# One PSUM tile per head pair for the first quad's transposes, a later first v load, and a last store from ScalarE's queue

## The chip, the cores and the metric

The kernel runs on one core of one Trainium2 chip. The metric is the device time of one execution in microseconds (us): three runs of the kernel before gave 442.17, 441.16 and 441.16, median 441.16. The profile is of one further execution, which took 439.23 us.

## The reference

Attention with a threshold, then a feed-forward layer that takes the largest of three products. Shapes: q, k, v are 8 batches x 8 heads x 576 rows x 64; the layer is 512 to 768 to 512.

```python
scores = scale * np.matmul(q, k.transpose(0, 1, 3, 2))
thresh = np.max(scores, axis=-1, keepdims=True) - tau
scores = np.where(scores >= thresh, scores, -1000000000.0)
attn = np.exp(scores - np.max(scores, axis=-1, keepdims=True))
attn = attn / (np.sum(attn, axis=-1, keepdims=True) + 1e-09)
x = np.matmul(attn, v)            # heads side by side: 4608 x 512
h = np.maximum(np.maximum(x @ w1, x @ w2), x @ w3)
out = h @ w_out
```

## The kernel before

The heads are taken four at a time, a *quad*: two quads per batch, 16 in all. A quad's q and k are loaded with 64 partitions for each of two heads (`load`, line 187); the four heads are a grid of `i` (upper or lower 64 partitions of the loaded tile) and `r` (first or second block of columns). For each quad TensorE transposes q and k (`transposed`, line 256; 64 x 64 pieces, five per `i` for `r` = 0, four for `r` = 1) into a PSUM tile `tp`; ScalarE copies q out with the scale into `qt`, VectorE copies k out into `kt`, and GpSimd makes `qs`, a copy of `qt` with upper and lower 64 partitions exchanged (`swapped`, line 242).

The work on scores goes by *chunks* of 128 query rows (nine per quad, `idx` 0 to 8) and by `r`. For one chunk and `r`: `scores` (line 287) makes 128 x 576 scores by matmuls on the upper and lower 64 rows of the array, `maximum` ("m", line 319, VectorE) finds the row's largest value, `exponents` ("e", line 331, ScalarE) makes the shifted values, and the numerators come from ScalarE ("n") or VectorE ("k") (line 339). A table `MASKED` says which chunks go the VectorE way; there "m" writes a copy `z` to SBUF, else "e" reads the scores in PSUM itself. Chunks 0 to 3 need only `i` = 0 of the transposed tiles, chunks 5 to 8 only `i` = 1 (chunk 4 both); chunks 0, 1, 5 and 6 read `qs` in its partitions 64 to 127 (the swap with x = 1), the others in partitions 0 to 63 (x = 0). The result is divided by the row sum (GpSimd), transposed by DMA (`ptq`), multiplied by v ("O"), and goes into the feed-forward layer ("F", "B") and out.

All PSUM is four tiles, s0 to s3, of two banks each (`bank`, line 183). Whatever is put into one of them has to wait until all readers of what was there before are done.

The order is written out by hand. Every engine's instructions are chained in program order (`_Ordered`, line 83), so an instruction that waits holds all behind it on its engine. `beginning()` (line 720) writes out the first quad; then the string `ORDER` (line 41) is followed letter by letter through `issue` (line 641): S0 to S3 is one chunk's `scores` in that tile, T a transpose of a later quad, "m", "e", "n", "k" as above, "a" and "c" the copies of a later quad's q and k out of PSUM, "q" its swaps, "l" one load, "g" and "z" load and cast of weights, "y" a cast of v, "o" a store. The first chunks are c0, c1 (both with `i` = 0; `r` = 0 of both comes before `r` = 1 of both), then c2 (`idx` 5).

In `beginning()` as it stands: 10 transposes of q for `r` = 0 into s0, 10 of k into s1, each tile holding both `i`, with the two `i` alternating. ScalarE copies q, VectorE k, one `i` at a time; three filling transposes keep TensorE busy (`FILL`); then the scores of c0 go to s0; then k and q of `r` = 1 into s2 and s3, all four of their copies by ScalarE; then the scores of c1 to s1. ORDER goes on with S2 and S3.

The first quad's loads are all issued first: on SyncE's queue q in three parts, then v (two of 256 KB, two of 32 KB); on ScalarE's queue k in three parts. The second quad's loads come with the letters "l" on SyncE's queue, behind v. At the end, the last "ninth" piece of the output (line 533) is copied out by VectorE and stored in two halves by SyncE; the store before it goes by ScalarE's queue (line 527).

Of the kernel before, what the change touches and what calls it, by code (L numbers as in the profile page):

```python
# [32 lines left out]
FILL = 3  # L33
# [8 lines left out]
lS2mS3mlemleS1neT0S2lmeamkmgllS1ekqlgT3T0qnalllncT0emS3cmlqqS2zenyyymS0ttzS1tS2eS3nemmnS0emlS2eememtekmS1eS3  # L42
kmgnltemS0S2eS1nklnmlktmS3gnS2eemS1RkmeT0metlmS2eleS3S1nkmmT3eazyS2emlD0ecmtbD3S1O0tkekmnbO2NRwS3wS1D0ennmqm
tebeS2D3bkS0T1ztmeaqkqO3nqtmneynO2NkwS1wS3nmS0F2S1mT3mgeBRmceD0klS3khebezS2tgF0S1mneBmlkmteD2vbF3S2T0kmBeS1n
aengvmezqS0F3mS2BS0mehrT1tS2neO3mecnnO1pgNttmF2qpkF0wwtrrkBT3zgyF1epaBnvvS3BlzhrS2mlF0RemkS1lnBlS2D3pvqD0pel
mrmppbklO3blO0teNqwpS1zweS2mS3npS0mmmrnF1BevS3T1emckS2emteS0npreptlnpT1S3kpmneptgarS2nmmeeS0pteS1mF3S0rekBmm
pnlpthlelS2kT3trktpS1epqpcmrF0nT3mtnpqpaBeS3S2evS0mF1yS3mnetmeegrBpF2mvT0crBeS1F3knpnhympzlgnenS0mlBqpeS1vmS
2O0O3erprmkNF1ekS2xwS3mmrnF0nqBpBepzplttvreS2ttpS3lptF1mmhnS0mBepzpeF3netrvnS2pmBS1pS0vnmtF2mS3S0rekepnepS1m
emreptBltkuS3upmmS0rF1lltpS2lnneekmmT3rBS0aS2kkueuepO3O1qlpqpmrpmekNeS0wmpxS2mF3F1rknBepeT0hplBcF2T3tnvT0Bta
S1ncF3qS0vBnmF2qyS1BemhrrkemF3S0nBvpF2pmepnpS1vBrmS0yeS3hemS2S1yylmlpF3plmmtleF0BlBkeetevrnF2T1T3vltoaBhT0tp  # L50
S1rapnknqS2F0cmmeS3BeF2pqS1mrBvpF0emS3ntppleBvrF2topytnS1kmmBS3hnS0O1vmlepnO2NeqmrkreeT3qS0xtptwcnnF2S1mmkF3
BlpveprBeS0lmS1ppF2hnmeS3rmpyBS1pnS0plvF3ntlT2mmeBaS1olevF2F3kmeueS2enrkrT0qT1tpBmakcepS1muS2urS0mopT3F1ntyp
pcS3leqkrenS2pppmmrneBS3memlupS0mS2uetetO1O3mnekrknpNwxS2S0S1pmpF3BemnF0mlqetS2kqreBtltpheF3knS1mBvprmF0vppe
S2nrBS3epnS1mrmmF2phS0BF1mveeF3kBS2epvenrBlnhnltS0mS1elolpmtltS3F0F2etypmmBkevyBpeT1rT3vF0ancS1BF2otnhmrS3BF
0kmtlplevrT1pppqpBtnltS2aS1oeT3rvmcS0nneS2meS3mqO1mmO0pppqeNeqkkreF2xwS3BS0pmpnhS1metnemF3F2lBkrlS1vBF0mrpve
npF3eBBhnkpvF2S1T0F3aurkBS0mltleS3rvS1mppmmlpqS2F0S1mtolnS2pqpteeemBrkneepS3ultuS1pmrmS2F0peepS3ymmkkntemeoB
nttS1rS2uuO3kppemmrkeO0leNS1xloT2T0npawS3mF1T0rclBcS2enmF0hprqqpmkeF1tpenBS3tttpntvmBoF2eS0vBmrS3S1yppmhS0mF
2eF3BBemepeF1nkT0vkrBF2vanhS0kBnF3F1mrBvBvppqS2petnS0prlpqrolmlmhnepS3F1mtltolBevleS2S0tmnnetF3pS1BmF0rmlepy
S2evBS3hmF1enT0pkBmcrppnvS2S3O0O1rmnNenpmeS3kxerwF2T1aT0mnBT3cvaF1S0ppBheqqprkplmS2eF3S1BmkvnF2eF0mkuqppBenl
S3S0vtrmtS1lmpprmpptF2S3lT0BtmttelteeocS3kekT1ruumS0aS2nmF1mkqrpS0enpeS3BermmkS2euS3pmuenS0qpO1mpyO2qmerekNp  # L60
xT0newS3cS2mleF1mF0BottpllykpBlhrtkF3pevF1BnnS2nvrmBS0mS3lhF2mpS1lotemyepeBpF0S3lvBnenF2tnS1BrkhmvpmtlypS3F0
F2eermkBBS1eF3vnnT0BrvpprrampypttltthS2S0mmS3emF1T0eS2T3cBpqS0mqS2nevemmyaeS3pmkeO1llktO0NpqpekeF2nxnlT3BF0c
rS3BwlvppmtrS1mnotoF2hS0enBmrpF1vrpqpF3lekBeBpnhF2S0vmT1tlpBS3lS0avmpF1tF2mBrnelekS3evutppmrS0qppS2nS1nmF3mr
mS2peekenpS0BemmeS1rkS2emuS0tlT1ueT3mcknrannpepF2S1mS3qppBmtotlmlttkrrpeueS1qqmS3lO0ueemoeO1opptpkklNwS2lS3x
F0mS1BnemehF2kT3mrcnpBS1F0rvS3BltlpnmF2nepmeveS1pkmBS0httnF3eF2mBrBekF1nS0vrBprvpypppS3nmhemeS2S1F3pF0mmBeBr
T2eS1kvnapS3vF2nS0mnBrmmreS3F1pheS2meeBqpnS0mvmeypS2tpS3etlO1qO0mNpmT3neytF2xtlkkrtnweS0ppT1cramBF3S1Bnehvpp
meS2rF0qqmT3BF1ncveT3ktnBF0vS2mrnarBhppS1lF3T0qppeBmcS1S2ovmF0mneT3naepBvS1S3enF0mkmrkqpqueenF2nS0tmS1T3cpqB
eupurrS3mmottoS0pS1mttneelotpmS2O3mkkO1rNwrpeexpneF0nkpS1S3S2mBemS1euuppmF2erkS3tltlBptmrF0S1lhtpmeyppBeS2mv
O1O3NenmxpS0S2kF1mxemrS3kBF2enF0vBermF1tBhpyppyektBvS2pmF3F0vBkS2BF1nmehS3vrBmtpO0eotpnevO2NkF1S3krmnrpxpxBh
F0S2eBF1mS3F2BnvpmBrS0vS3S1ehemmF2kppmnF0rBvkBF3F1BF2ehBtkvevoF3pptkttO0O1NuprBwS3xS1vmmpeS0ekF2S3pmF1oeBmrB  # L70
okettF0peuokoruoF3uhF2pkkF0hvvruF3pF2F0hppF1pvvF3F2vvF0F1F3hvtovhtF2F0F1F3htvF2voF0O1uvO3NvF2xwF0hF3F1vF0vhF
3F1F0hvF3vvF1F0F3vF1hF0hovF3vF1F0vhF3vvF1vBuuF0BuouoF3uooo
# [31 lines left out]
def kernel(  # L104
# [82 lines left out]
    def load(g, first=False):  # L187
# [276 lines left out]
    def ffn(b, part):  # L464
# [68 lines left out]
        def ninth():  # L533
# [10 lines left out]
            def done():  # L544
# [47 lines left out]
    warm = bank("warm", 3)  # L592
# [41 lines left out]
    line["D"] = [(g, r, part) for part in range(2) for g in range(2) for r in range(2)]  # L634
# [85 lines left out]
    def beginning():  # L720
# [38 lines left out]
        for r in range(2):  # L759
            for x in (1, 0):  # L760
                swap(r, 1, x)
# [45 lines left out]
```

## Time and profile before

| | us |
|---|---|
| median of three runs | 441.16 |
| the profiled execution | 439.23 |
| its span | 437.1 |
| TensorE matmuls busy | 420.2 |
| VectorE busy | 398.9 |
| ScalarE busy | 386.1 |
| GpSimd busy | 289.8 |
| first transpose of q | 4.41 |
| first scores | 6.19 |

Times in the profile are counted from the start of the span; the execution has 2.1 us more around it. PE is TensorE's matmuls, PEld its weight loads, DVE VectorE, ACT ScalarE, POOL GpSimd, SP SyncE; a q behind the name is the engine's own instruction queue, which issues DMAs. In a timeline row the first number is the start, the second the length, then engine, operation, output and inputs, and xN the number of instructions that were merged into the row; a bracket gives the idle time before it and what ended it. Nearly every row has line 92, which is the helper that records instructions, so rows are told apart by their tiles.

### The profile page before, as it was taken

What the parts mean: (1) busy time and instruction counts of PE and PEld (TensorE: products, weight loads), DVE (VectorE), ACT (ScalarE), POOL (GpSimd) and SP (SyncE); (2) the same over time, 40 slices, a digit from 0 to 9 for tenths busy, and PEclk for the clock granted to TensorE, in tenths of its full rate; (3) what the DMA queues carried; (4) which work ended last, traced back from release to release, by engine and by line L of the source; (5) the groups of instructions that cost most, each with busy time, mean ns of one, the idle gap of its engine ahead of it and who ended that gap; (6) DMA issues with size and microseconds to landing.
All of it is one profiled execution on the core that took longest, in us unless ns stands there. A gap on an engine that the chain in (4) does not pass through costs nothing.

```text
span 437.1 us, 14271 instructions
## 1 busy us (share of the span) xinstructions
PE 420.2 (96%) x5313; PEld 305.8 (70%) x5313; DVE 398.9 (91%) x1109; ACT 386.1 (88%) x780; POOL 289.8 (66%) x370
## 2 busy tenths in 40 slices
PE   7769998899999999999999999999999999999995
PEld 5535776567787767767787767777677776777862
DVE  3999999999999999999999999999999999999641
ACT  5999989999999999999999999989999999875422
POOL 3614487898879697577668779768769677554500
PEclk9999999999999999999999999999999999999999
DMA  8999999999999999999999969999999977574602
GB/s 256 306 237 219 294 225 209 237 241 205 184 237 212 229 222 207 201 231 221 196 199 206 213 146 253 175 192 218 237 195 183 222 143 145 120 161 125 177 14 109
DMA packets 212773, 87.45 MB, mean 200 GB/s; under 512 B 185824, under 2 KB 199648, under 8 KB 212704
## 3 DMA queue, kind: packets, MB, share of 16 engines
q1 hardware_dynamic: 212000, 85.69, 94.7%
q8 instruction: 42, 0.69, 0.7%
q10 hardware_dynamic: 704, 0.85, 0.6%
q14 instruction: 27, 0.22, 0.2%
HBM read 34.60 MB, written 9.44 MB: 101 GB/s over the span
## 4 chain that ended last, share of the span: by engine, by line
PE 84%; ACT 6%; DVE 5%; issue 2%; DMA 2%; ACTq 0%; DVEq 0%
PE ph L92 32%; PE sc L92 28%; PE po L92 11%; PE o L92 8%; ACT z L92 4%; PE tp L92 4%; DVE z L92 2%; DVE unused L92 1%; ACT P L92 1%; DMA km<-in_k_dram 1%; DMA qm<-in_q_dram 1%; DVE P L92 1%; ACT qt L92 1%; PE d L92 0%; DVE kt L92 0%
## 5 line engine op out<-in xcount | busy, mean ns | idle before, releaser
L92 POOL TENSOR_SCALAR P<-z,rs 128x576 bf16<-128x576 f32 x252 | 207.5, 837 | 77.7 <-DVE rs L92 34.6
L92 PE MATMUL sc<-kt,qt 64*128 64x256 f32 (+2 forms) x640 | 179.5, 422 | 4.2 <-DVE z L92 2.0
L92 PE MATMUL sc<-kt,qs 64*128 64x320 f32 (+2 forms) x640 | 177.4, 411 | 3.0 <-ACT z L92 1.3
L92 PE MATMUL ph<-xt,w 64*128 64x288 bf16 (+4 forms) x2160 | 171.9, 283 | 0.2
L92 PEld LDWEIGHTS <-w 64*128 64x128 bf16 (+1 forms) x2160 | 124.2, 94 | 34.9 <-issue 7.2
L92 DVE TENSOR_SCALAR_CACHE_REDUCE unused<-sc 128x576 bf16<-128x576 f32 x168 | 123.9, 750 | 4.2 <-PE sc L92 3.1
L92 ACT ACTIVATE z<-sc,nm 128x576 f32<-128x576 f32 x168 | 121.7, 743 | 3.9 <-DVE unused L92 1.5
L92 PEld LDWEIGHTS sc<-kt,qs 64*128 64x128 f32 (+1 forms) x640 | 90.6, 175 | 19.9 <-ACT z L92 7.1
L92 PEld LDWEIGHTS sc<-kt,qt 64*128 64x128 f32 (+1 forms) x640 | 90.3, 175 | 18.5 <-ACT z L92 5.7
L92 ACT ACTIVATE z<-z 128x576 f32<-128x576 f32 x148 | 100.4, 682 | 0.3
L92 ACT ACTIVATE z<-z,nm 128x576 f32<-128x576 f32 x120 | 91.3, 774 | 4.7 <-DVE z L92 4.4
L92 DVE TENSOR_SCALAR_CACHE_REDUCE z<-sc 128x576 f32<-128x576 f32 x120 | 89.3, 752 | 5.1 <-PE sc L92 3.7
L92 DVE SCALAR_TENSOR_TENSOR z<-z 128x576 f32<-128x576 f32 x104 | 81.0, 789 | 0.1
L92 POOL COPY qs<-qt 64x640 f32<-64x640 f32 (+3 forms) x68 | 48.0, 706 | 25.8 <-ACT qt L92 22.5
L92 PE MATMUL po<-wo,hT 64*128 64x512 bf16 (+1 forms) x480 | 53.6, 357 | 0.1
L92 ACT ACTIVATE hm<-ph 128x576 bf16<-128x576 f32 (+4 forms) x54 | 32.1, 595 | 20.0 <-PE ph L92 19.6
L92 DVE TENSOR_TENSOR hm<-ph,hm 128x576 bf16<-128x576 f32 (+4 forms) x54 | 36.9, 684 | 7.9 <-PE ph L92 7.9
L92 PEld LDWEIGHTS <-hT 64*128 64x128 bf16 (+1 forms) x480 | 26.5, 97 | 19.7 <-issue 3.4
L92 DVE TENSOR_TENSOR hT<-ph,hm 128x576 bf16<-128x576 f32 (+4 forms) x54 | 37.1, 687 | 2.3 <-PE ph L92 0.4
L92 PE MATMUL o<-ptq,vb 128*64 128x64 bf16 (+2 forms) x576 | 35.8, 275 | 0.0
L92 PEld LDWEIGHTS <-vb 128*64 128x64 bf16 x576 | 22.5, 111 | 14.9 <-issue 5.8
L92 ACT ACTIVATION_READ_ACCUMULATOR z<-z 128x1 f32 x148 | 29.5, 199 | 0.0
(40 smaller groups left out, 298.4 us busy)
## 6 DMA issues: line engine op xcount, KB each, us to landing
vm<-in_v_dram SPq DMA_DIRECT2D x32, 256.0 KB, 5.1
out_dram<-ob SPq DMA_DIRECT2D x31, 256.0 KB, 3.1
qm<-in_q_dram SPq DMA_DIRECT2D x15, 512.0 KB, 4.8
km<-in_k_dram SPq DMA_DIRECT2D x15, 512.0 KB, 5.5
stage<-in_moe_w_dram SPq DMA_DIRECT2D x9, 512.0 KB, 5.3
ptq<-P SPq DMA_TRANSPOSE x144, 4.3
stage<-in_moe_w_out_dram SPq DMA_DIRECT2D x3, 512.0 KB, 5.3
qm<-in_q_dram SPq DMA_DIRECT2D x16, 64.0 KB, 3.4
```

Of the source, the lines that this page charges most:

```text
L92: ins = fn(*a, **kw)
```

## The change

1. `beginning()` fills a PSUM tile of its own for each of q and k and each `i` for `r` = 0: q and k of `i` = 0 into s2 and s3, q and k of `i` = 1 into s0 and s1; five transposes each, one `i` after the other. Then the scores of c0 and c1 follow one another (s2 and s3), and the first "m" is issued. Then q of `r` = 1 goes into s1 and k of `r` = 1 into s0, again `i` = 0 before `i` = 1. Their copies alternate with "e" of c0 and "m" of c1. All k copies are VectorE's now; before, ScalarE made the two of `r` = 1. The four x = 1 swaps come before the four x = 0 swaps.
2. `ORDER` has the same letters, without the "m", "m", "e" that `beginning()` now issues, and with the tiles renamed throughout (0 with 2, 1 with 3). So its first score, c0 with `r` = 1, goes to s0, the next, c1 with `r` = 1, to s1.
3. The three filling transposes and `FILL` are gone; the warming transposes use s1 instead of s3.
4. The third part of the first q goes by ScalarE's queue, that of k by SyncE's. The first v (four DMAs) is issued behind the second quad's q and k.
5. Of the last two half stores one goes by ScalarE's queue.

```diff
-        for n, src, e in srcs:
+        for n, src, e in (srcs if not first else (("q", q, q2), ("k", k, sync))):
             if first:
                 e.dma_start(out=L[n][:, 10:18], in_=rows_of(src)[:, 1, 0:8])
...
                     for x in range(2):
-                        sync.dma_start(out=rows_out[:, 8, 256 * x:256 * x + 256], in_=ob[64 * x:64 * x + 64])
+                        e = scalar if x == 0 and b == B - 1 else sync
+                        e.dma_start(out=rows_out[:, 8, 256 * x:256 * x + 256], in_=ob[64 * x:64 * x + 64])
...
-    warm = bank("warm", 3)
+    warm = bank("warm", 1)
...
+    first_loads = load(0, first=True)
+
+    def later_loads():
+        for g in range(1, NQ):
+            for n, _ in enumerate(load(g)):
+                if g == 1 and n == 3:
+                    for _ in first_loads:
+                        pass
+                yield
...
-                 l=(None for g in range(1, NQ) for _ in load(g)))
+                 l=later_loads())
...
-        def turn(n, r, where):
-            p = transposed(L, n, r)
-            p.first(where)
-            ps[n, r] = p
+        def turn(n, r, i, to):
+            rows = slice(64 * i, 64 * i + 64)
+            main = to[:, 0:256].rearrange("p (jj u x) -> p jj x u", jj=2, x=2)
+            for j in range(5 - r):
+                tensor.transpose(main[:, j // 2, j % 2] if j < 4 else to[:, 256:320],
+                                 couple(L, n, r, j, rows), identf[rows, rows])
+            ps[n, r, i] = to
 
         def copy(n, r, i):
-            ps[n, r].half(i, scalar if n == "q" or r else vector)
+            dst, src = L[n + "t"][:, i, 320 * r:320 * r + 64 * (5 - r)], ps[n, r, i][:, 0:64 * (5 - r)]
+            if n == "q":
+                scalar.activation(out=dst, in_=src, func=AF.Copy, scale=scale)
+            else:
+                vector.tensor_copy(out=dst, in_=src)
...
-        turn("q", 0, 0)
-        copy("q", 0, 0)
-        swap(0, 0, 1)
-        turn("k", 0, 1)
-        copy("k", 0, 0)
-        copy("q", 0, 1)
-        copy("k", 0, 1)
-        swap(0, 0, 0)
-        for _ in range(FILL):
-            tensor.transpose(warm[:, 0:128], identf, identf)
-        issue("S", 0)
-        turn("k", 1, 2)
-        copy("k", 1, 0)
-        turn("q", 1, 3)
-        copy("q", 1, 0)
-        swap(1, 0, 1)
-        copy("k", 1, 1)
-        copy("q", 1, 1)
-        issue("S", 1)
-        swap(1, 0, 0)
-        for r in range(2):
-            for x in (1, 0):
-                swap(r, 1, x)
-
-    for _ in load(0, first=True):
-        pass
+        for i, where in ((0, (2, 3)), (1, (0, 1))):
+            for n, w in zip("qk", where):
+                turn(n, 0, i, bank("tp", w))
+                copy(n, 0, i)
+                if n == "q" and i == 0:
+                    swap(0, 0, 1)
+        swap(0, 1, 1)
+        issue("S", 2)
+        issue("S", 3)
+        issue("m", None)
+        for n, w in (("q", 1), ("k", 0)):
+            to = bank("tp", w)
+            for i in range(2):
+                turn(n, 1, i, to[:, 512 * i:512 * i + 512])
+        for i in range(2):
+            copy("q", 1, i)
+            swap(1, i, 1)
+            copy("k", 1, i)
+            if i == 0:
+                issue("e", None)
+                issue("m", None)
+        for r in range(2):
+            for i in range(2):
+                swap(r, i, 0)
+
+    for _ in range(4):
+        next(first_loads)
     beginning()
```

More of the change, by code (lines that the diff above doesn't have):

```diff
@@ L72 @@
-3F1F0hvF3vvF1F0F3vF1hF0hovF3vF1F0vhF3vvF1vBuuF0BuouoF3uooo
+lS0S1lmleS3neT2S0lmeamkmgllS3ekqlgT1T2qnalllncT2emS1cmlqqS0zenyyymS2ttzS3tS0eS1nemmnS2emlS0eememtekmS3eS1kmg
+nltemS2S0eS3nklnmlktmS1gnS0eemS3RkmeT2metlmS0eleS1S3nkmmT1eazyS0emlD2ecmtbD1S3O2tkekmnbO0NRwS1wS3D2ennmqmteb
+eS0D1bkS2T3ztmeaqkqO1nqtmneynO0NkwS3wS1nmS2F0S3mT1mgeBRmceD2klS1khebezS0tgF2S3mneBmlkmteD0vbF1S0T2kmBeS3naen
+gvmezqS2F1mS0BS2mehrT3tS0neO1mecnnO3pgNttmF0qpkF2wwtrrkBT1zgyF3epaBnvvS1BlzhrS0mlF2RemkS3lnBlS0D1pvqD2pelmrm
@@ new lines @@
+ppbklO1blO2teNqwpS3zweS0mS1npS2mmmrnF3BevS1T3emckS0emteS2npreptlnpT3S1kpmneptgarS0nmmeeS2pteS3mF1S2rekBmmpnl
+pthlelS0kT1trktpS3epqpcmrF2nT1mtnpqpaBeS1S0evS2mF3yS1mnetmeegrBpF0mvT2crBeS3F1knpnhympzlgnenS2mlBqpeS3vmS0O2
+O1erprmkNF3ekS0xwS1mmrnF2nqBpBepzplttvreS0ttpS1lptF3mmhnS2mBepzpeF1netrvnS0pmBS3pS2vnmtF0mS1S2rekepnepS3memr
+eptBltkuS1upmmS2rF3lltpS0lnneekmmT1rBS2aS0kkueuepO1O3qlpqpmrpmekNeS2wmpxS0mF1F3rknBepeT2hplBcF0T1tnvT2BtaS3n
+cF1qS2vBnmF0qyS3BemhrrkemF1S2nBvpF0pmepnpS3vBrmS2yeS1hemS0S3yylmlpF1plmmtleF2BlBkeetevrnF0T3T1vltoaBhT2tpS3r
@@ L73 @@
+ttF2peuokoruoF1uhF0pkkF2hvvruF1pF0F2hppF3pvvF1F0vvF2F3F1hvtovhtF0F2F3F1htvF0voF2O3uvO1NvF0xwF2hF1F3vF2vhF1F3
+F2hvF1vvF3F2F1vF3hF2hovF1vF3F2vhF1vvF3vBuuF2BuouoF1uooo
 """
```

51 lines of the change are left out of this document (20 added, 31 removed).

## The prediction

> **What bounds the kernel now.** I read the page's busy times first, then its chain that ended last, then the chain piece by piece over the first 14 us, because the change is all in the start and the last store.
>
> ```profile
> PE 420.2 (96%) x5313; PEld 305.8 (70%) x5313; DVE 398.9 (91%) x1109; ACT 386.1 (88%) x780; POOL 289.8 (66%) x370
> ...
> PE 84%; ACT 6%; DVE 5%; issue 2%; DMA 2%; ACTq 0%; DVEq 0%
> ```
>
> ```profile
> 0.00:10.00 10.00, 7.95 (x73) 6.31 (x73) 3.11 (x9) 4.77 (x10) 3.39 (x13) 1.00 0.81 244
> 10.00:20.00 10.00, 7.44 (x79) 5.25 (x76) 9.61 (x27) 9.85 (x22) 7.88 (x11) 1.00 1.12 319
> 20.00:30.00 10.00, 6.45 (x55) 3.32 (x54) 10.00 (x32) 10.00 (x21) 1.32 (x3) 1.00 1.09 243
> ```
>
> The second fence is the table by stretches: us, then busy time of PE, PEld, DVE, ACT and POOL. TensorE is the bound of the whole, but not of the start: VectorE and ScalarE are full from about 10 us on, and TensorE, with 7.4 and 6.5 of 10 us, waits for them. So what the change does to the moment at which these two engines become full is what it does to the end, one for one, unless something between absorbs it.
>
> ```profile
> 1.65 5.05 DMA km<-in_k_dram
> ...
> 6.71 4.45 DMA qm<-in_q_dram
> ...
> 11.30 0.54 PE tp L92 x10
> ...
> 11.86 0.70 ACT qt L92
> ```
>
> This is the chain's start. Its first engine step is the second quad's transposes, held by a load that was issued only at 6.71. It reads as if an earlier load would pay directly. The rows of the engines say how much:
>
> ```profile
> 5.10 0.77 ACT L92 ACTIVATE qt<-tp 128x320 f32<-128x320 f32 x2 [1.65 <-PE tp L92]
> 7.28 0.39 ACT L92 ACTIVATE kt<-tp 128x256 f32<-128x256 f32 x1 [1.41 <-PE tp L92]
> 7.56 0.38 ACT L92 ACTIVATE qt<-tp 128x256 f32<-128x256 f32 x1
> ...
> 8.35 0.77 ACT L92 ACTIVATE z<-sc,nm 128x576 f32<-128x576 f32 x1
> 8.97 0.80 ACT L92 ACTIVATE z<-z,nm 128x576 f32<-128x576 f32 x1
> ...
> 10.31 1.40 ACT L92 ACTIVATE z<-sc,nm 128x576 f32<-128x576 f32 x2
> 11.86 0.70 ACT L92 ACTIVATE qt<-tp 128x640 f32<-128x640 f32 x1 [0.15 <-PE tp L92]
> 12.46 0.77 ACT L92 ACTIVATE z<-z,nm 128x576 f32<-128x576 f32 x1
> ```
>
> ```profile
> 5.41 0.89 DVE L92 COPY kt<-tp 128x320 f32<-128x320 f32 x2 [5.41 <-PE tp L92]
> 7.03 0.76 DVE L92 TENSOR_SCALAR_CACHE_REDUCE unused<-sc 128x576 bf16<-128x576 f32 x1 [0.73 <-PE sc L92]
> 8.13 0.76 DVE L92 TENSOR_SCALAR_CACHE_REDUCE z<-sc 128x576 f32<-128x576 f32 x1 [0.33 <-PE sc L92]
> ...
> 9.30 0.76 DVE L92 TENSOR_SCALAR_CACHE_REDUCE unused<-sc 128x576 bf16<-128x576 f32 x1 [0.41 <-PE sc L92]
> 9.99 0.75 DVE L92 TENSOR_SCALAR_CACHE_REDUCE unused<-sc 128x576 bf16<-128x576 f32 x1
> ...
> 12.44 0.76 DVE L92 TENSOR_SCALAR_CACHE_REDUCE unused<-sc 128x576 bf16<-128x576 f32 x1 [0.33 <-PE sc L92]
> 13.26 0.76 DVE L92 SCALAR_TENSOR_TENSOR P<-z 128x576 bf16<-128x576 f32 x1
> ...
> 15.35 0.69 DVE L92 COPY kt<-tp 128x512 f32<-128x512 f32 x1
> 15.96 0.75 DVE L92 TENSOR_SCALAR_CACHE_REDUCE unused<-sc 128x576 bf16<-128x576 f32 x1
> ```
>
> ScalarE sat idle only 0.15 us for that late load (11.86), VectorE 0.33 (12.44). VectorE's waits after its first maximum are 0.33 + 0.41 + 0.33, and about 0.06 at 13.26: 1.1 us in all. From 13.26 on it is full.
>
> **The change part by part.** I lay out the first quad anew with these durations.
>
> *Transposes of r = 0, a tile for each head pair.*
>
> ```profile
> 4.79 0.28 PE L92 MATMUL tp<-identf,qm 64*128 64x64 f32 x2
> 4.90 0.48 PE L92 MATMUL tp<-identf,km 64*128 64x64 f32 x10
> ...
> 5.30 0.55 PE L92 MATMUL warm<-identf 128*128 128x128 f32 x3
> ...
> 5.69 0.96 POOL L92 COPY qs<-qt 64x320 f32<-64x320 f32 x2 [4.38 <-ACT qt L92]
> ...
> 6.19 0.48 PE L92 MATMUL sc<-kt,qs 64*128 64x256 f32 x1 [0.33 <-POOL qs L92]
> ...
> 6.57 0.43 PE L92 MATMUL sc<-kt,qt 64*128 64x320 f32 x1
> ...
> 6.74 0.50 PE L92 MATMUL tp<-identf,km 64*128 64x64 f32 x8
> ...
> 8.45 0.53 PE L92 MATMUL sc<-kt,qs 64*128 64x320 f32 x1 [0.36 <-POOL qs L92]
> ...
> 9.84 0.38 PE L92 MATMUL sc<-kt,qs 64*128 64x256 f32 x1
> ```
>
> Ten transposes of k took 0.48, of which the last one's own length is about 0.22 (estimate: 0.28 for the two of the row above, less a little): nine steps in 0.26. They alternate between the array's halves. If a pair starts together, one half takes 0.064 per transpose; if the halves simply share, any sequence runs at 0.03; a transpose of the full array, twice as wide, took (0.55 - 0.27)/2, at most 0.14, and I take 0.11 for the upper end since the first of the three is the longest. The values 0.03, 0.064 and 0.11 are the bounds and my choice; 0.064 is the reading of the same instruction, so it is nearest. In the new order five on one half follow one another, so that is the pace.
>
> The Trainium skill, TensorEngine Tiling (Array Packing), Key Properties, says that tiles operate independently and that different tiles load and multiply in parallel; it speaks against this change, since neighbours in the queue now lie on the same half. By that rule the delay below is +0.8; without it (0.03 in any order) it would be +0.45. No row separates the halves cleanly, but the even pairs of ten in 0.48 agree with it.
>
> The first q copy gains nothing: the last two transposes of q start only at 4.79, behind the small second load, and one of these two is needed for i = 0. So q of i = 0 is complete at 5.06 as now, its copy starts at 5.10, the swap at 5.69, and the first scores at 6.19, unchanged. The other 15 transposes end by 4.85 + 15 x 0.064 + 0.22 = 6.0, beside the copy and the swap. The fillers lie in the same shadow (0.55 from 5.30): taking them away gives nothing.
>
> *The scores of c0 and c1 together, then r = 1.* A score of c0 takes from 6.19 to 7.00 and its maximum starts at 7.03, as now. Three scores in a row took 8.45 to 10.22, one of them 0.80, so each further one 0.49: c1's are complete at 7.49 instead of 8.09. But VectorE's order is now maximum c0, k copy, maximum c1, k copy. The transposes of r = 1 start 0.26 before the score ahead of them ends (6.74 against 7.00), so at 7.25. The k transposes of i = 0 are numbers 9 to 12: last one complete at 7.25 + 11 x 0.064 + 0.22 = 8.17. k copy 1 starts at 8.21. A copy of 512 columns takes 0.61 from start to start (15.35 to 15.96), of 320 about 0.41, so 256 takes 0.34 (estimate). Maximum c1 starts at 8.55 (now 8.13), k copy 2 at 9.22, done at 9.6.
>
> What is queued behind: the first score of ORDER, c0 with r = 1, goes to s0, where both k halves of r = 1 lie, so TensorE waits for k copy 2 and starts at 9.65 (now 8.45, behind the swap). All of TensorE's later scores are queued behind it. Its maximum follows 0.85 later (8.45 to 9.30), at 10.50: VectorE idles about 0.9, and is 1.20 late.
>
> ScalarE: the two k copies go (0.27 each, 7.28 to 7.56: 0.54), but it isn't earlier for that. "e" of c0 r = 1 follows its maximum by 0.84 (8.13 to 8.97): 11.34, now 10.31. "e" of c1 r = 1: maximum 10.50 + 0.68 = 11.18, so 12.02. The copy of the second quad's q: 12.02 + 0.62 (8.35 to 8.97) = 12.64, now 11.86: **+0.78**. Its transposes don't wait any more, so 0.15 of idle is saved in this. VectorE: maxima and one numerator at 11.86 and 12.53, next maximum at 13.20 (now 12.44, +0.76), then its numerator waits for "e" at 12.64 + 0.60 + 0.80: 14.04 (now 13.26, +0.78). Both engines are then full, and 0.8 late. With the pace at 0.03 the same sum gives +0.45.
>
> *The loads.*
>
> ```profile
> vm<-in_v_dram SPq DMA_DIRECT2D x4, 256.0 KB, 5.8
> ...
> 16.97 1.04 POOL L92 CAST vb<-vm 128x1024 bf16<-128x1024 f32 x1
> ```
>
> Seven SP issues stand ahead of the second quad's; four of them (v) move behind, and about as many issues stand ahead of the weights as before. The second quad's q is issued between 3 and 6.7 and lands by 11.16 at the latest; it is needed at 11.4 or later. v is then issued by about 7.5 and lands 5.8 later, 13.3, ahead of GpSimd's cast at 16.97, which hides it; without that cover GpSimd would cast late, and the products with v would wait. The third parts of q and k swap queues at the same place in each: the k part landed at 6.70, and the transposes of r = 1 now start at 7.25. Cost nothing; range 0 to 0.3, if SyncE's queue gets that much later.
>
> *The swaps.* x = 1 of i = 1 is GpSimd's second, ready by 6.7, before c2 wants it. The x = 0 swaps go behind; chunks 2 and 3 come much later. Nothing.
>
> *The last store.*
>
> ```profile
> 433.08 0.66 ACTq L92 DMA_DIRECT2D out_dram<-ob  x1
> 433.22 1.43 SPq L92 DMA_DIRECT2D out_dram<-obr  x2
> ```
>
> SyncE issues two halves until 434.65. Then it issues one, and ScalarE's queue the other, behind its own store, from 433.74 to about 434.4. Between 0 and -0.25; I take -0.2, the difference of these ends.
>
> *Sum.* +0.8 - 0.2 = **+0.6**. The profiled execution would take 439.23 + 0.6 = 439.8; the median of the runs stands 1.9 above it, so 441.16 + 0.6 = **441.8**, 0.14% slower. What a measurement of this kernel can tell from no change is about 0.3%, 1.3 us.
>
> **The rivals.** *A, as above:* +0.6, own range +0.1 to +1.5.
>
> *B, the transposes on one half run at 0.11.* For it: the full-array row, whose successive loads and multiplies also meet on the same cells. Against it: k's ten in 0.48. The 15 behind the first q end later, and the first scores start at 4.79 + 16 x 0.11 = 6.55 (+0.36); k of r = 1 is copied at 9.08, maximum c1 at 9.42, k copy 2 at 10.09, the score in s0 at 10.53, its maximum at 11.38, the second quad's q at 13.52: +1.66, less 0.2: +1.5, so 442.7. It is over 1.3 from a pace of about 0.1.
>
> *C, the wait for s0 isn't there* (k copy 2 done before 8.4): then the earlier load gives up to 0.15 + 0.15 on ScalarE, and with the store -0.5: 440.7. Against it: two copies and a maximum on one in-order engine, after 8.17.
>
> *D, the delay is absorbed before the end:* only the store counts, 441.0. Against it: the chain has no DMA behind 11.16.
>
> *E, over 1.3 faster.* All VectorE waits up to 13.26 are 1.1, and its two new copies take 0.68 of them; 0.45 + 0.25 at the end is the most that these rows hold. It would need a gain further on that they don't show, such as fewer collisions of loads with the transposing DMAs between 14 and 40 us: about 439.5.
>
> **How the numbers follow.** A 0.50 (0.36 within 0.3%, 0.14 above), B 0.28 (0.26 above), C 0.06, D 0.06, E 0.10. So slower 0.40, the same 0.50, faster 0.10. The range goes from C's 440.7 to 443.3, B with 0.3 from the loads and 0.3 for its pace; A's own is 441.2 to 442.7.
>
> **What would show it.** First scores at 6.2; maximum c1 at 8.5; the scores of c0 r = 1 held by DVE kt until about 9.65, and VectorE idle some 0.9 ahead of that maximum; no wait for the load at the second quad's transposes, whose q copy starts at 12.6; the cast of v without a wait. Wrong would be: first scores well off 6.19, transposes of one half that run at another pace, or a later stretch (20 to 50 us) in which VectorE or ScalarE have idle time that they don't have now.

## The result, and the profile after

| | before | after |
|---|---|---|
| median of 22 runs each, taken together | 441.08 us | 442.17 us |
| lowest and highest | 439.46 to 444.42 | 440.52 to 445.81 |
| the profiled execution | 439.23 | 441.46 |
| its span | 437.1 | 439.4 |

The ratio is 1.0039, with a 95% interval from 1.0022 to 1.0055: the changed kernel is slower, by 0.4%. The medians lie 1.1 us apart, the ratio times 441.08 is 1.7 us, and the two profiled executions differ by 2.2. The pair of profiles therefore shows the loss somewhat larger than the runs do on average, since the profiled execution before (439.23) is faster than all of its 22 runs; I use the pair to find places, and the runs to size them. Of the experiments below, single runs that took far longer than the rest (847.53, 706.65, 484.25 and 450.58 us, and two of 1471 us of the kernel before) are left out of the ratios, but not of the medians.

The busy times of the page of the changed kernel look almost as before:

```profile
PE 420.9 (96%) x5310; PEld 307.3 (70%) x5310; DVE 400.5 (91%) x1111; ACT 386.1 (88%) x778; POOL 287.8 (66%) x370
```

VectorE has 1.6 us more, ScalarE the same, and GpSimd 2.0 less. Where that matters is seen only by laying the rows of both kernels beside each other. VectorE at the start, after the change (start, length, operation, idle time before it):

```profile
8.29 0.42 DVE L91 COPY kt<-tp 128x256 f32<-128x256 f32 x1 [0.33 <-PE tp L91]
8.63 0.75 DVE L91 TENSOR_SCALAR_CACHE_REDUCE z<-sc 128x576 f32<-128x576 f32 x1
...
9.31 0.42 DVE L91 COPY kt<-tp 128x256 f32<-128x256 f32 x1
10.72 0.76 DVE L91 TENSOR_SCALAR_CACHE_REDUCE unused<-sc 128x576 bf16<-128x576 f32 x1 [1.00 <-PE sc L91]
```

TensorE and then ScalarE in the same stretch:

```profile
5.50 0.47 PE L91 MATMUL tp<-identf,km 64*128 64x64 f32 x5
6.35 0.48 PE L91 MATMUL sc<-kt,qs 64*128 64x256 f32 x1 [0.38 <-POOL qs L91]
...
9.87 0.51 PE L91 MATMUL sc<-kt,qs 64*128 64x320 f32 x1 [1.62 <-POOL qs L91]
...
11.38 0.54 PE L91 MATMUL tp<-identf,qm 64*128 64x64 f32 x10
```

```profile
12.84 0.69 ACT L91 ACTIVATE qt<-tp 128x640 f32<-128x640 f32 x1
```

The chain is the predicted one. The second k copy comes behind the maximum of c1 (9.31), the first score into s0 starts only at 9.87, VectorE idles 1.00 for it, and the copy of the second quad's q starts at 12.84 instead of 11.86. Counted from the first maximum, that copy stood 4.83 behind it (7.03 to 11.86) and now stands 5.64 behind it (that maximum started at 7.20, so 7.20 to 12.84): **+0.81, predicted +0.78**. The other 0.17 was there before the first maximum: the first transposes began at 4.54 instead of 4.41, behind the warming transposes, which ended later though they began at the same time (before, then after):

```profile
1.36 3.12 PE L92 MATMUL warm<-identf 128*128 128x128 f32 x14 [1.36 <-POOL identf masks.py:199]
```

```profile
1.36 3.25 PE L91 MATMUL warm<-identf 128*128 128x128 f32 x14 [1.36 <-POOL identf masks.py:199]
```

The second quad's transposes (11.38) no longer wait. The page puts the wait of 1.62 down to GpSimd's swap; the first experiment shows that it is the k copy.

So far 1.0 us. The rest is lost in a place where I expected nothing. VectorE between 34 and 39 us, before and then after:

```profile
34.45 0.75 DVE L92 SCALAR_TENSOR_TENSOR P<-z 128x576 bf16<-128x576 f32 x1
...
35.13 0.76 DVE L92 SCALAR_TENSOR_TENSOR P<-z 128x576 bf16<-128x576 f32 x1
...
36.49 0.20 DVE L92 RECIPROCAL scales<-sums 128x8 f32<-128x8 f32 x1
```

```profile
35.43 1.38 DVE L91 SCALAR_TENSOR_TENSOR P<-z 128x576 bf16<-128x576 f32 x1
...
36.74 1.26 DVE L91 SCALAR_TENSOR_TENSOR P<-z 128x576 bf16<-128x576 f32 x1
...
38.61 0.19 DVE L91 RECIPROCAL scales<-sums 128x8 f32<-128x8 f32 x1
```

The first of these two numerators is 0.98 late, as the q copy was. Then the same two instructions take 1.38 and 1.26 us instead of 0.75 and 0.76, and the reciprocal behind them is 2.12 late (36.49 to 38.61). Nothing shows as idle: the loss sits in the busy time of VectorE, and the table by stretches calls it 10.00 of 10 us busy there in both kernels. What lies beside them is GpSimd's work (`stage` is where a load of weights lands, and the cast turns it into `w`), before and then after:

```profile
33.30 0.72 POOL L92 COPY qs<-qt 64x640 f32<-64x640 f32 x1 [3.12 <-ACT qt L92]
35.48 1.30 POOL L92 CAST w<-stage 128x1024 bf16<-128x1024 f32 x1 [1.47 <-DMA stage<-in_moe_w_dram]
36.85 0.72 POOL L92 COPY qs<-qt 64x640 f32<-64x640 f32 x1
```

```profile
34.38 0.72 POOL L91 COPY qs<-qt 64x640 f32<-64x640 f32 x1 [3.94 <-ACT qt L91]
35.16 1.04 POOL L91 CAST w<-stage 128x1024 bf16<-128x1024 f32 x1
36.27 1.12 POOL L91 COPY qs<-qt 64x640 f32<-64x640 f32 x1
```

One rule fits all these lengths: of two such instructions the one that started first runs its normal length, and the one that started second is stretched by the overlap less about 0.13 us. Before, the cast began at 35.48, behind the second numerator (35.13 to 35.89): overlap 0.41, less 0.13 is 0.28, and the cast took 1.30 instead of 1.04; VectorE lost nothing. After, the cast began at 35.16, ahead of the first numerator (35.43): it ended at 36.20, overlap 0.77, less 0.13 is 0.64, and the numerator took 1.38 instead of 0.75. The swap that began at 36.27 was now second to that numerator (until 36.81) and took 1.12 instead of 0.72; being first to the next numerator by its start at 36.27, it stretched that one by 37.39 - 36.74 - 0.13 = 0.52. So one collision made the next. The cast after the change has no wait of its own: its load had landed, and it followed at once on the swap of 34.38, which had waited for ScalarE. Before, it waited 1.47 for its load.

The Trainium skill, SBUF — State Buffer, section "Who interferes with whom", states that VectorE and GpSimd share one pair of ports under an exclusive lock, that a VectorE instruction with two SBUF inputs contends with a GpSimd instruction that reads SBUF, and that the order of issue decides which of them blocks. These rows agree, with 0.63 and 0.51 us on VectorE's side after the change and 0.26 on GpSimd's before it. The profile before was lucky in this more than once: two later casts came second as well, and GpSimd paid (1.41 at 47.61 and 1.58 at 51.43, instead of 1.04).

From there VectorE stays 2.0 to 2.1 late up to 130 us (a reciprocal at 130.61 before stands at 132.70 after). At 133 to 135 us it is up to 2.8 late, by a wait of 0.38 for TensorE and by a third such numerator (1.10 instead of 0.74 at 133.99, beside GpSimd's multiplications from 133.01 on). Most of this is given back: at 247 us it is 2.34 (a reciprocal at 247.47 and 249.81).

The queues of SyncE and of ScalarE at the end of the changed kernel:

```profile
435.53 0.55 SPq L91 DMA_DIRECT2D out_dram<-obr  x1
```

```profile
436.11 0.62 ACTq L91 DMA_DIRECT2D out_dram<-obr  x1
```

From the first of the last output matmuls (po) to the end of the span it was 427.58 to 437.1 = 9.5 us before, and is 429.89 to 439.4 = 9.5 after. The two half stores now stand in two queues, but ScalarE's issue (436.11) began only when SyncE's had ended (436.08). The last issue ends at 436.73, 6.84 behind that matmul, where it was 434.65, 7.07 behind. These 0.23 do not show at the end.

The account of the profiled pair: 0.17 + 0.81 + 1.14 (the numerators: 2.12 less 0.98) = 2.12, of 2.3 in the span; the other 0.2 is what is left of the rise and fall behind 130 us.

### The profile page after: what moved, and what is told of

Same layout as the page of the kernel before. It is cut to its first block, busy times and chain, and to the rows that moved or that the text cites. A ratio compares the mean times of both kernels' runs of the same rounds, so it can differ in the third digit from the quotient of the medians.

```text
span 439.4 us, 14265 instructions
## 1 busy us (share of the span) xinstructions
PE 420.9 (96%) x5310; PEld 307.3 (70%) x5310; DVE 400.5 (91%) x1111; ACT 386.1 (88%) x778; POOL 287.8 (66%) x370
## 4 chain that ended last, share of the span: by engine, by line
PE 85%; ACT 6%; DVE 5%; issue 2%; DMA 1%; POOL 0%; DVEq 0%; SPq 0%; POOLq 0%; ACTq 0%
PE ph L91 32%; PE sc L91 29%; PE po L91 11%; PE o L91 8%; ACT z L91 4%; PE tp L91 4%; DVE z L91 2%; ACT P L91 1%; DVE unused L91 1%; ACT qt L91 1%; PE warm L91 1%; PE d L91 1%; DMA out_dram<-ob 1%; DVE P L91 0%; DVE hT L91 0%
## 5 line engine op out<-in xcount | busy, mean ns | idle before, releaser
L91 DVE COPY kt<-tp 128x640 f32<-128x640 f32 (+3 forms) x34 | 24.3, 718 | 6.3 <-PE tp L91 6.1
```

What stands on the lines that cost most here:

```text
L91: ins = fn(*a, **kw)
```

## The experiments

Three readings of the start and of the loss at 35 us had to be told apart, and the expectations call them by letters: K, that the second k copy holds the first score of r = 1; G, that GpSimd's swaps hold it, as the page says; and P, that the delay of 1 us moves the numerators into GpSimd's casts, so that the end pays twice (other letters in the expectations are explained there). Each kernel was timed beside the kernel before on the same chip; n is its number of runs.

**Both k copies ahead of the maximum of c1**, all else as in the changed kernel:

```diff
-                issue("m", None)
+        issue("m", None)
```

(the maximum leaves the loop over the two k copies and follows it)

> The kernel after, with both k copies of r = 1 ahead of the maximum of c1 on VectorE; nothing else moves. Theory K (the first score of r = 1 waits in tile s0 for the second k copy): k copies at 8.3 and 8.6, the score starts at about 9.1 in place of 9.87, its maximum at 10.0 in place of 10.72, the copy of the second quad's q at 12.4 in place of 12.84: 0.4 to 0.7 us gained. Rival G (it waits for GpSimd's second swap, which the profile names): the score stays at 9.8 to 9.9 and nothing is gained. What the later numerators at 35 us do depends on their overlap with GpSimd, so the whole time is open to about 1 us more or less.

Measured: ratio 0.9998, 95% 0.9972 to 1.0023 (median 440.93, n 9), span 438.8. VectorE:

```profile
8.24 0.76 DVE L91 COPY kt<-tp 128x256 f32<-128x256 f32 x2 [0.33 <-PE tp L91]
...
9.99 0.76 DVE L91 TENSOR_SCALAR_CACHE_REDUCE unused<-sc 128x576 bf16<-128x576 f32 x1 [0.33 <-PE sc L91]
```

The maximum behind the score in s0 moved from 10.72 to 9.99, though the swaps are where they were (8.43 and 9.34, after the change 8.48 and 9.39), and the score itself started at 9.14 with DVE kt named as its releaser. K holds and G is out. The q copy came at 12.30, 5.15 behind the first maximum (7.15), so 0.49 of the 0.81 is the order of one maximum and one copy. The numerators (34.92, 35.60) then took 0.75 each and the cast, which came behind them at 35.72, took 1.53: GpSimd paid. Two things decided this: the numerators came half a microsecond earlier than in the changed kernel, and the cast had to wait 1.16 for its load. This profile paid elsewhere:

```profile
47.82 1.61 DVE L91 SCALAR_TENSOR_TENSOR P<-z 128x576 bf16<-128x576 f32 x1
```

```profile
47.78 1.04 POOL L91 CAST w<-stage 128x1024 bf16<-128x1024 f32 x1 [2.86 <-DMA stage<-in_moe_w_dram]
```

Here the cast was first by 0.04 us, and the numerator lost 0.86. So the span is 1.7 longer than that of the profile before, although the runs of the two kernels are level.

**The kernel before with a later start.** Eighteen fillers instead of three, which delays its start without any other part of the change:

```diff
-FILL = 3
+FILL = 18
```

> The kernel before with 18 filling transposes in place of 3, about 1.1 us more of TensorE ahead of the first score, so all computing starts about as late as in the kernel after (the copy of the second quad's q at about 12.8, +1.0) with the loads as they were. Theory P: GpSimd's cast at 35.5 comes when its load lands and not with the computing, so it now meets the numerators, which come 1.0 later; the reciprocal behind them is 1.5 to 2.1 later than 36.49, and so is the end. Rival S (a late start is handed through as it is): 1.0 later there and at the end, numerators at 0.75.

Measured: ratio 1.0021, 95% 0.9995 to 1.0047 (441.96, n 10), span 439.9, which is 2.8 more than before. VectorE and GpSimd:

```profile
35.54 1.42 DVE L92 SCALAR_TENSOR_TENSOR P<-z 128x576 bf16<-128x576 f32 x1
...
36.88 1.25 DVE L92 SCALAR_TENSOR_TENSOR P<-z 128x576 bf16<-128x576 f32 x1
```

```profile
35.31 1.04 POOL L92 CAST w<-stage 128x1024 bf16<-128x1024 f32 x1 [0.21 <-DMA stage<-in_moe_w_dram]
36.41 1.12 POOL L92 COPY qs<-qt 64x640 f32<-64x640 f32 x1
```

Its q copy was 1.04 late (12.90), and at 35 us the same collision happened to the same instructions, within 0.04 us of the lengths in the changed kernel; the reciprocal came at 38.75, 2.26 late. The second loss thus does not need the new tiles, the loads or the store: a delay of 1 us by another means brings it too. That is P, for this profile; the interval of its runs still takes in 1. A third collision (a numerator at 51.65 took 1.44, beside a cast that began at 51.43) makes up 0.7 of its 2.8.

**The cast in question replaced by a fill with zeros**, in the changed kernel, so that GpSimd only writes there (one block of weights is left out of the computation):

```diff
+                if blank:
+                    pool.memset(dst, 0.0)
+                else:
...
```

> The kernel after, but the fourth piece of weights is not cast: GpSimd writes zeros into it in place of the cast, so this kernel leaves part of the layer's first weights out. In the profile after, VectorE's two numerators at 35.43 and 36.74 took 1.38 and 1.26 us in place of 0.75, while GpSimd's cast (35.16) and a swap (36.27) ran. Theory P (the two engines can't both read SBUF by a shared port, whoever starts first holds it): a GpSimd instruction that only writes doesn't hold it, both numerators take 0.75, the reciprocal behind them starts at 37.5 in place of 38.61, and the span is 0.8 to 1.2 shorter than the profile after (439.4). Rival D (the numerators are slow because data or loads arrive late): they stay at 1.2 to 1.4 and nothing changes after them.

Measured: 1.0046, 95% 1.0022 to 1.0070 (443.38, n 10), span 441.0: no gain. GpSimd and VectorE:

```profile
36.76 0.95 POOL L91 MEMSET w<- 128x1024 bf16 x1
37.77 0.71 POOL L91 COPY qs<-qt 64x640 f32<-64x640 f32 x1
```

```profile
37.13 0.75 DVE L91 SCALAR_TENSOR_TENSOR P<-z 128x576 bf16<-128x576 f32 x1
...
37.81 1.28 DVE L91 SCALAR_TENSOR_TENSOR P<-z 128x576 bf16<-128x576 f32 x1
```

The mechanism is clear and the expectation of the time failed. The numerator beside the fill took 0.75, so an instruction that only writes does not hold VectorE; the next one lost 0.53, because the swap now began 0.04 us ahead of it. Taking one collision away handed the place to another. And this execution was late for a second reason, which its TensorE rows show:

```profile
5.83 0.74 PE L91 MATMUL tp<-identf,km 64*128 64x64 f32 x5
6.55 0.76 PE L91 MATMUL sc<-kt,qs 64*128 64x256 f32 x1
```

```profile
6.00:8.00 2.00, 2.00 (x13) 1.81 (x12) 0.89 (x2) 0.44 (x1) 0.86 (x2) 1.00 1.02 328
```

Its first scores take 0.76 instead of 0.48, its transposes are up to 0.107 apart instead of 0.062, the first maximum comes at 8.02 and the q copy at 14.55. The array ran at half its pace, although the clock column of the stretches (the third number from the end) reads 1.00. Why it does is told below.

**The kernel before with only the loads and the store of the change:**

```diff
-        for n, src, e in srcs:
+        for n, src, e in (srcs if not first else (("q", q, q2), ("k", k, sync))):
...
-                  l=(None for g in range(1, NQ) for _ in load(g)))
+                  l=later_loads())
...
+                        e = scalar if x == 0 and b == B - 1 else sync
```

> The kernel before with the change's loads (q's and k's third part on the other queue, first v behind the second quad's q and k) and its last store; order of all computing as before. Theory of the prediction: no wait for the load at the second quad's transposes, the copy of that quad's q at 11.56 to 11.7 in place of 11.86, so 0.15 to 0.3 us gained, and the store gives 0 to 0.25 from the last matmuls to the end. Rival L (the chain's own reading: the late load is what sets the start): the 1.08 us that TensorE waited are gained. Rival 0: neither gives anything.

Measured: 0.9978, 95% 0.9954 to 1.0002 (440.51, n 6), span 437.6. TensorE:

```profile
7.35 0.46 PE L92 MATMUL tp<-identf,km 64*128 64x64 f32 x8
...
10.62 0.48 PE L92 MATMUL tp<-identf,qm 64*128 64x64 f32 x10
```

The second quad's transposes start at 10.62 without a wait, and still the q copy comes at 12.12, again 4.83 behind the first maximum (7.29): the transposes of r = 1 start at 7.35 instead of 6.74, since their loads landed later in this execution, and that takes back what the wait gave. It is not shown to be the edit's doing: by the traces the last of the third parts landed at 6.81 to 7.37 in the four profiles with the old loads and at 6.58 to 7.31 in the ten with the new ones. The loads are worth about nothing, as predicted, though in this profile for a reason that the prediction did not have. This is the fastest kernel that was measured, and its interval still touches 1.

**The changed kernel with the loads of before:**

```diff
-        for n, src, e in (srcs if not first else (("q", q, q2), ("k", k, sync))):
+        for n, src, e in srcs:
...
-    for _ in range(4):
-        next(first_loads)
+    for _ in first_loads:
+        pass
```

> The kernel after with the loads of the kernel before (v of the first quad ahead of the second quad's, third parts on their former queues). Theory of the prediction (the loads cost and gain nothing here, since the start is held by the k copies): the copy of the second quad's q follows the first maximum by 5.6 us as in the kernel after (7.20 to 12.84; before: 7.03 to 11.86, 4.83), time within 0.15% of the kernel after. Rival L2: the early loads of the second quad hold back the third parts of the first (the transposes of r = 1 began at 7.35 with the new loads and the old order, 6.74 before), so the old loads start r = 1 earlier and the time falls by 0.1 to 0.3%.

Measured: 1.0039, 95% 1.0012 to 1.0065 (442.81, n 12). The ratio is that of the changed kernel: the loads are not its loss. Its profiled execution (446.4) was another with the array at half pace, up to 17.7 us, its q copy at 15.54.

**Shorter casts against the collisions.** If a second instruction waits for the rest of the first, casts cut into two or four pieces should cost the numerator less. This was tried in the changed kernel, in the kernel with both k copies first, and in the kernel before with the new loads and store:

```diff
-                pool.tensor_copy(out=dst, in_=my["t"].rearrange("p (k f) -> p k f", k=src.shape[1]))
+                t = my["t"].rearrange("p (k f) -> p k f", k=src.shape[1])
+                for x in range(src.shape[1]):
+                    pool.tensor_copy(out=dst[:, x], in_=t[:, x])
```

> The kernel after, with each cast of weights cut into two or four GpSimd instructions (256 columns, about 0.26 us each, in place of one of 1.04). Theory P (VectorE's two-input instruction waits for the GpSimd instruction that has started, and no longer): the two numerators near 35.4 lose at most about 0.15 each to the cast, so 0.3 in place of 1.14 where only the cast stands in the way, and the kernel is 0.5 to 1 us faster than the kernel after, 0.1 to 0.2% above the kernel before. Rival D (something else makes them slow): unchanged, 0.4% above before.

> Both k copies of r = 1 ahead of the maximum of c1, and the casts cut. From the two effects by themselves: start 0.45 behind the kernel before, at most 0.3 more to the casts up to 50 us, so between the kernel before and 0.2% slower; 0.1 to 0.3% under a_kfirst if that kernel's numerators lost 0.85 to a cast at 47.8 as its profile shows.

> The kernel before with the change's loads and store, and the casts cut. Theory P: VectorE's numerators lose 0.23 + 0.24 + 0.17 to casts in the profile of the same kernel with whole casts; cut ones leave less than 0.2 of it, so 0.2 to 0.3% faster than the kernel before. Rival: the casts cost as much in pieces, and it stays where the kernel with whole casts was (0.9978).

Measured, in this order: 1.0031 (1.0009 to 1.0053, 443.14, n 12), 1.0032 (1.0008 to 1.0056, 442.98, n 12) and 0.9988 (0.9970 to 1.0007, 441.24, n 12). None is measurably faster than its uncut sibling. In the first profile the load of the cast landed late, the two numerators at 35.66 and 36.34 took 0.75 by that chance, and VectorE waited 0.98 for a DMA at 41 us instead; the second was again at half pace at the start (q copy 14.86). There the cut casts did meet the two numerators (pieces from 37.42 on), and these took 0.75 and 0.94, 0.19 lost in place of about 1.1: at this place the cut did what was expected, but the runs don't show it. The middle one also warns against taking 0.9998 for the kernel with both k copies first as settled: it contains that edit, and 4 of its 12 runs lie above 443.4, against 1 of 9.

**The array's pace.** Three profiles of the changed kernel's kind (fill with zeros, old loads, k first with cut casts) had half the pace in their scores and three (the changed kernel, k first, cut casts) had not; none of the four with the old transposes and their fillers had it. The change also takes the fillers away and lets five transposes follow each other on one half of the array.

How long the half pace lasted can be read from the clock records that each trace keeps, which the views only average. No record stands ahead of the first grant of the full clock, and where none stands the view subtracts nothing: that is the 1.00. Counted from the start of the span, the first record begins at 10.40 (fill with zeros), 14.13 (k first with cut casts) and 17.68 us (old loads); in the other eleven profiles, those of the last four kernels below among them, it begins between 4.18 and 6.22 (4.21 before, 4.99 after the change). The rows agree: with the old loads a score of 256 columns still took 0.63 at 16.82, and from 17.68 on a transpose takes 0.23 instead of 0.31.

All records but the last of a trace, which the end cuts off, are 3.413 us or a multiple of it long, so in these traces the clock changes only at steps of this length. Counting back from the three late records in such steps gives 3.57, 3.89 and 4.03. So a step up to 4.03 did not bring the full clock and one from 4.18 on did, while TensorE's first instruction stood at 1.36 in all of them: what sorts these fourteen profiles is the moment of the step. That this moment is chance, and not set by the kernel, is likely, since all of them start alike up to there, but it is not shown. None of the five profiles of the kernel before and its variants had a step between 3.57 and 4.03, so they don't tell whether the fillers would have helped there.

Four kernels were made to tell these apart: the kernel before without fillers, and the changed kernel with three fillers, with transposes that alternate between the halves in four tiles of their own, and with both and the k copies first.

```diff
-FILL = 3
+FILL = 0
```

> The kernel before without its three filling transposes. Theory F: the array stays at half pace at the start in some executions, a quarter or more of the times above 443 (2 of 81 above 443.4 so far), median 0.1 to 0.3% up. Rival H (transposes that alternate between the halves are enough to open the clock): as the kernel before, ratio 1.000 within its interval, no time above 443.4. Prediction's own: nothing changes, since the fillers lie beside the copy and the swap.

```diff
+        for _ in range(3):
+            tensor.transpose(ps["k", 0, 1][:, 512:640], identf, identf)
```

> The kernel after with three filling transposes of the full array behind the 20 of r = 0, as the kernel before has them. In three of the six profiles so far with the change's transposes the array ran at half pace at the start: transposes 0.107 apart in place of 0.062, the first scores' matmuls 0.76 long in place of 0.48, and this lasted to between 11 and 16 us; in none of four profiles with the old transposes and the fillers. Theory F (the fillers open the clock): first scores' matmuls 0.48 long, times above 443.4 in at most 1 of 12 (8 of 22 in the kernel after), median 441.5 to 442. Rival H (what counts is that transposes fill half of the array at a time): as the kernel after, a third of the times above 443.4. Rival Z (chance of the moment): no kernel differs.

```diff
-        for i, where in ((0, (2, 3)), (1, (0, 1))):
-            for n, w in zip("qk", where):
-                turn(n, 0, i, bank("tp", w))
+        for n, where in (("q", (2, 0)), ("k", (3, 1))):
+            turn(n, 0, [bank("tp", w) for w in where])
```

(`turn` then writes one transpose of each half in turn)

> The kernel after with its own four tiles, but the transposes of the two head pairs alternate between the halves of the array as in the kernel before; no fillers. Theory H: half pace is gone, at most 1 of 12 times above 443.4, median 441.3 to 441.8; the start's own delay stays (the copy of the second quad's q 5.5 behind the first maximum, 4.83 before). Theory F: a third of the times above 443.4, as in the kernel after.

> The kernel after with all three: both k copies of r = 1 ahead of the maximum of c1, alternating transposes, and three fillers. If the delay of the k copies and the slow start of the array are the whole loss, the start is 0.2 to 0.5 behind the kernel before (the copy of the second quad's q 5.1 behind the first maximum), no time is above 443.4, and the ratio is between 0.999 and 1.0015. If it stays at 1.003 or more, something else costs, such as GpSimd's casts meeting VectorE.

Measured: without fillers 1.0021 (0.9995 to 1.0048, 442.41, n 12); with three fillers 1.0060 (1.0035 to 1.0084, 443.78, n 12); alternating 1.0021 (0.9999 to 1.0043, 442.51, n 12); all together 1.0049 (1.0024 to 1.0074, 443.32, n 12). The hoped-for repair failed, and the first reason is in how I placed the fillers. TensorE of the kernel with three fillers:

```profile
7.04 0.55 PE L91 MATMUL tp<-identf 128*128 128x128 f32 x3 [0.58 <-DVE kt L91]
7.52 0.48 PE L91 MATMUL sc<-kt,qs 64*128 64x256 f32 x1
```

They write into the second bank of a tile whose first bank VectorE is copying out, so they waited for that copy and stood ahead of the first scores, which came at 7.52 instead of 6.35. These two kernels therefore say nothing on the fillers. In both profiles the same two numerators met the cast again (1.31 and 1.26 us with the fillers alone, 1.31 and 1.25 with all together). The kernel before without fillers does: its k transposes came in pairs, one on each half, 0.107 apart, its first scores came at 6.54, and later its clock fell, here the stretches 16 to 18 and 34 to 36 us (clock third from the end):

```profile
16.00:18.00 2.00, 2.00 (x11) 1.90 (x13) 1.75 (x6) 2.00 (x5) 1.93 (x2) 0.62 1.56 350
...
34.00:36.00 2.00, 2.00 (x17) 1.14 (x18) 1.54 (x4) 1.76 (x3) 0.72 (x1) 0.50 0.94 275
```

Its scores took 0.63 and 0.74 there, the lengths of the half pace at the start of the other profiles, VectorE waited for them, and its numerators at 36.65 and 38.07 met the cast as well. But mean clocks as low as that execution's 0.988 also occur among the runs of the kernel before, so this is no proof that the missing fillers cause it. The alternating kernel had the full pace (first scores 6.48, 0.48 long) and only 2 runs above 443.4, where the changed kernel has 8 of 22; it still had the wait for the k copy (VectorE 1.00 at 10.79) and lost 0.83 at a numerator (36.17, 1.58 long) beside a cast (35.58, 1.56 long). This cast was itself stretched by the numerator before (35.50 to 36.25), and the rule gives both lengths: 36.25 - 35.58 - 0.13 = 0.54 for the cast, 37.14 - 36.17 - 0.13 = 0.84 for the numerator.

## Why the prediction was right where it was, and where it was not

The time, 442.17 against 441.8, lies inside the range, and the sign was that of the likeliest case; yet the ratio lies just beyond 0.3%, in the part that had a chance of 0.4, and not for the reasons of the sum. That the forecast lies within 0.4 us is in part luck: the start has the size that the sum gave it, the store gave nothing, and in the profiled pair collisions that the sum lacks cost more than the start.

| step of the prediction | predicted | profile after |
|---|---|---|
| transposes on one half, each | 0.064 | 0.062 (five of k in 0.47, the last 0.22 long) |
| first scores | 6.19 | 6.35 |
| k copy 1, maximum c1, k copy 2 | 8.21, 8.55, 9.22 | 8.29, 8.63, 9.31 |
| first score in s0, its maximum | 9.65, 10.50 | 9.87, 10.72 |
| q copy of the second quad | 12.64 | 12.84 |
| the same, behind the first maximum | 5.61 | 5.64 |
| second quad's transposes | no wait | no wait |
| first cast of v | no wait | 17.93, no wait |
| last store | -0.2 | 0 |

*The start.* Each step came where it was put, all shifted by the first one, and k-first showed on the chip that the copy holds the score. Case C (no wait for s0) is refuted; so is D, since nothing absorbed the delay, and so is E, since the kernel is not faster. (The collisions of loads with transposing DMAs that E named are not what changed.) The first scores were 0.16 late because the first transposes began 0.13 later. That is not the change's doing: 4.53 or 4.54 also stands in four profiles of the kernel before with other edits, while their first load had landed at 4.14 to 4.47, always behind warming transposes that took 3.25. The profile of the kernel before was the early one: its full clock came at 4.21, and its warming transposes took 3.12.

*The step that failed* is "what the change does to the moment at which these two engines become full is what it does to the end, one for one, unless something between absorbs it". I thought of absorption alone. Before, the weight cast came when its load had landed, the numerators when the computing had got there; a delay of the computing alone moved the two against each other. Here it turned a collision that GpSimd paid (0.26, free) into two that VectorE paid (1.14). It is more than the chance of one delay: in a later start the cast no longer waits for its load but follows on a swap, which comes with the computing. By the q copy, the changed kernel is 0.98 late, and the profiles with all together, with three fillers and with the old loads are 1.26, 2.15 and 3.68 late; in all four the cast stands right behind the swap, and the two numerators lost 1.14, 1.06, 1.07 and 1.13. Where it still waited a little for its load (eighteen fillers, 1.04 late, and alternating, 1.05 late) they lost 1.17 and 0.83. The prediction looked for "idle time that they don't have now"; there is none, because a blocked instruction counts as busy. The lengths of single instructions were the thing to watch. With the smaller delay of k-first (0.44) GpSimd still paid at this place.

*"Taking them away gives nothing"*, on the fillers, and case B: the half pace of 0.107 exists, as B's price had it, but not as the cost of one half. On one half the transposes went at 0.062 when the array was at its full pace and at 0.107 when it wasn't; the alternating ones of the kernel without fillers went at 0.107 for a pair. So B's number came for another reason, the array's pace. When the full clock first came went with the moment of the 3.41 us step in all fourteen profiles; whether the fillers or the order of the transposes decide how long a late start lasts **stays open**. The fillers of the kernel before stand behind the transposes, so they can't set the pace of these; they could set how soon it ends. The three profiled executions at half pace in their scores took 443.1, 444.2 and 446.4 us (those at full pace 440.9, 441.5 and, with the late load, 443.9), and the runs of the changed kernel's kind above 443.4 are frequent (8 of 22, against 1 of 22 of the kernel before beside it). That fits, but the unprofiled runs show no rows, so this part of the 1.7 us is argued and not shown.

*The store* was mis-sized: -0.2 for the last issue ending earlier, and 0 at the end. The issue did end 0.23 earlier; the end didn't follow it. *The loads* came to nothing: the second quad's transposes no longer wait, as foreseen, and in the one profile with the loads alone a late landing of the third parts (7.35 instead of 6.74 for the transposes that need them) took that back.

## What to carry to other kernels

When a change delays one chain by a microsecond, ask which other chain keeps its own time (here casts at the landing of loads) and which engine pairs disturb each other; the price of the delay is set where the two meet again, and can double it. Look for that price in the lengths of single instructions, not in idle time. In an in-order engine, put the copy that a tile's next user waits for ahead of the maximum that nobody waits for so urgently: that order alone was worth 0.5 us of the 0.8 in the profile here.

## What the runs showed of the hardware that I had not expected

A VectorE instruction with two inputs and a GpSimd instruction that reads stretch each other by nearly a fixed rule: the second to start is longer by the overlap less about 0.13 us, the first not at all (0.77 gave 0.63, 0.65 gave 0.51, 0.41 gave 0.26, 0.67 gave 0.53 and 0.52). In the trace of the kernel before, 120 such VectorE instructions have 576 columns; 31 of them began beside an earlier GpSimd instruction with more than 0.13 us left. The rule gives the length of 27 within 0.02 us; the other four (59.56, 395.18, 403.95, 405.77) kept their 0.73 to 0.75 us, each beside a GpSimd instruction that was itself longer than usual. None of the other 89 is longer than 0.76. A fill with zeros on GpSimd did not stretch its neighbour (0.75).

The granted clock of the views reads 1.00 ahead of the first clock record, while matmuls run at half pace: 0.76 instead of 0.48 for the same first scores, up to the records at 10.40, 14.13 and 17.68 us in three executions. The Trainium skill, TensorE: Matmul & The Clock Gate, Part 1, says that the array starts at half its clock and is released after a busy window of about 3.4 us whose phase differs from run to run. The steps of 3.413 us and the half pace up to 4.2 to 6.2 us in eleven executions agree with that. A half pace up to 17.68, 16.3 us behind TensorE's first instruction, is longer than one such window; the records show when the full clock was granted there, and no run shows what kept it back until then.
